# A channel gate that is guessed early: flag and branch ahead of ScalarE's last waits, an early gate from 44 rows, four slots of 68 rows, 512-wide sums

## The chip, the cores and the metric

The kernel runs on one core of one Trainium2 chip. The metric is the device time of one execution in microseconds, as the median of ten runs; beside them stands one profiled execution, whose trace is read here.

## The reference

`x` has the shape 1 x 384 x 384 x 384 (height, width, channels) in bf16, `w1d` has one element. Cut to what matters, for a one-element filter:

```python
g = jnp.einsum("bhwc->bc", x) / (H * W)     # mean of each channel
s = sigmoid(g * w1d[0])                     # one gate per channel
return x * s[:, None, None, :]              # every pixel times its channel's gate
```

The mean needs all of `x`, and the product needs all of `x` again: 113.25 MB are read and 113.25 MB written if `x` is read once.

## The kernel before, in words

**Guess, then check.** A core's on-chip memory does not hold `x`. The kernel therefore computes a gate `s_early` from the first rows alone, multiplies every row with it as the rows pass through, and goes on summing. At the end it computes the true gate `s_true` from the sum of everything and compares both as bf16 bit patterns (`not_equal`, a maximum over the channels, a cast to the integer `redo`). If they differ anywhere, a second pass reads `x` again and multiplies with `s_true`. With these inputs they are the same, and the second pass is branched over.

**Rows and tiles.** A "row" is 128 pixels, one to a partition, with 384 channels in each: 768 bytes per partition. There are 1,152 rows. They are cut into 26 tiles, eight of 45 rows and eighteen of 44 (`split(n_rows, TILE)`). A tile's transfer has one contiguous piece per partition (34,560 or 33,792 bytes), so 128 pieces, which are shared by the core's 16 DMA engines. Partition p holds pixels that follow each other in memory.

**The arena.** What is left of the on-chip memory, 209,344 bytes per partition or 272 rows, is the arena. The class `Ring` hands out places in it one after the other; six tiles fit. A tile that needs a place in use first has the oldest tile gated and stored (`put`).

**What each engine does for a tile.**
- SyncE issues the load (`load`, through `plan.dma`, line 91).
- TensorE adds the rows up over the partitions: one matmul per row with a matrix of ones, 384 columns wide, accumulated in one PSUM bank (`add_rows`, line 206): bank `acc0` for the first three tiles, `acc1` for the others.
- VectorE multiplies the tile in place with the gate (`gate`, line 165).
- ScalarE issues the store (`put`, through `plan.dma`).

After the third tile VectorE copies the sum to `total` (line 249) and ScalarE computes `s_early` (line 255). After the last tile's gate VectorE adds the second bank (line 267), ScalarE computes `s_true` (line 273), and VectorE makes the flag (lines 281, 289, 295).

**Order and waits.** The class `Planner` writes one stream of instructions for each engine, in the order in which `plan.op` and `plan.dma` are called, and puts in the waits: before an operation the engine waits for the writer of what it reads, and for the writer and readers of what it overwrites (line 99). Each DMA has a semaphore of a pool of 50. An engine works through its stream in that order. So where a step stands in the code decides what stands ahead of it in its engine's stream.

**The end.** SyncE, VectorE and ScalarE each call `second_pass`: wait for the flag, load it into a register (line 326), branch (line 327). ScalarE first waits for all stores (lines 345 and 346) and raises `stored`, for which the other engines would wait inside the branch. Line 322 stands for the block's end, where all engines meet.

Of the kernel before, what the change touches and what calls it, by code (L numbers as in the profile page):

```python
# [3 lines left out]
P = 128  # L4
ROW = 384
BF16 = mybir.dt.bfloat16
F32 = mybir.dt.float32
U16 = mybir.dt.uint16
I32 = mybir.dt.int32
ACT_F = mybir.ActivationFunctionType  # L10
ALU = mybir.AluOpType


class Planner:
# [9 lines left out]
    def __init__(self, nc, name, n_dma_sems):  # L24
        self.nc = nc
        self.streams = {e: [] for e in ("sync", "scalar", "vector", "tensor", "gpsimd")}
        self.sems = {e: nc.alloc_semaphore(f"{name}_{e}") for e in self.COMPUTE}
        self.count = {e: 0 for e in self.COMPUTE}
        self.pool = [nc.alloc_semaphore(f"{name}_dma_{i}") for i in range(n_dma_sems)]
        self.pool_uses = [0] * n_dma_sems  # L30
        self.n_dma = 0
        self.writer = {}
        self.readers = {}
        self.seen = {e: {} for e in self.streams}
        self.final = []
# [70 lines left out]
def split(n, most):  # L106
    k = -(-n // most)
    return [n // k + (i < n % k) for i in range(k)]


class Ring:


    def __init__(self, size):
        self.size, self.at = size, 0

    def take(self, n):
        if self.at + n > self.size:
            self.at = 0
        self.at += n  # L120
        return self.at - n


TILE = 45
AHEAD_TILES = 3


def bass_standalone__channel_attn_eca__vision_kernel(
# [3 lines left out]
    out: bass.AP,  # L132
):
    B, H, W, C = x.shape
    assert B == 1 and C == ROW and (B * H * W) % P == 0
    n_rows = B * H * W // P
    x_rows, o_rows = x.flatten_outer_dims(), out.flatten_outer_dims()

    def dram(view, r0, n):
        return view[r0 * P : (r0 + n) * P, :].rearrange("(p t) c -> p (t c)", p=P)  # L140

    ones = nc.alloc_sbuf_tensor("ones", [P, P], BF16)
    s_early = nc.alloc_sbuf_tensor("s_early", [P, C], BF16)
    s_true = nc.alloc_sbuf_tensor("s_true", [P, C], BF16)
    w_one = nc.alloc_sbuf_tensor("w_one", [1, 16], BF16)
    w_scaled = nc.alloc_sbuf_tensor("w_scaled", [P, 2], F32)
    warm = nc.alloc_sbuf_tensor("warm", [P, 2], F32)
    wrong = nc.alloc_sbuf_tensor("wrong", [P, 1], F32)
    redo = nc.alloc_sbuf_tensor("redo", [P, 1], I32)
    total = nc.alloc_sbuf_tensor("total", [P, C], F32)  # L150
    n_arena = nc.sbuf_bytes_remaining // (2 * C)
    arena = nc.alloc_sbuf_tensor("arena", [P, n_arena * C], BF16)
    acc = [nc.alloc_psum_tensor(f"acc{i}", [P, 512], F32) for i in range(3)]

    def at(r0, n):
        assert r0 + n <= n_arena
        return arena[:, r0 * C : (r0 + n) * C]

    def rows(r0, n):
        return [("sb", r) for r in range(r0, r0 + n)]  # L160

    def gate(place, n, s):
        s_b = s[:].unsqueeze(1).broadcast_to([P, n, C])
        v = at(place, n).rearrange("p (t c) -> p t c", t=n)
        return lambda e: e.tensor_tensor(v, v, s_b, ALU.mult)  # L165

    sizes = split(n_rows, TILE)
    early_rows = sum(sizes[:AHEAD_TILES])
    plan = Planner(nc, "a", 50)


    plan.op("gpsimd", lambda e: e.memset(warm[:, 0:1], 0.0), writes=["warm"])  # L172
    plan.op("vector", lambda e: e.memset(ones[:], 1.0), writes=["ones"])  # L173
    plan.dma("scalar", w_one[0:1, 0:1], w1d.unsqueeze(0), writes=["w_one"])
    plan.op(
        "scalar",
        lambda e: e.activation(warm[:, 1:2], warm[:, 0:1], ACT_F.Sigmoid),  # L177
        reads=["warm"],
        writes=["warm1"],
    )  # L180
    plan.op(
        "tensor",
        lambda e: e.matmul(  # L183
            acc[2][:, 0:1], ones[0:1, :], w_one[0:1, 0:1], start=True, stop=True
        ),
        reads=["ones", "w_one"],
        writes=["acc2"],
    )
    for i, n in enumerate((early_rows, n_rows)):
        plan.op(  # L190
            "vector",
            lambda e, i=i, n=n: e.tensor_scalar_mul(  # L192
                w_scaled[:, i : i + 1], acc[2][:, 0:1], 1.0 / float(P * n)
            ),
            reads=["acc2"],
            writes=[f"w_scaled{i}"],
        )

    def load(place, n, r0):
        plan.dma("sync", at(place, n), dram(x_rows, r0, n), writes=rows(place, n))  # L200

    def add_rows(place, n, bank, first, last):
        for i in range(n):
            plan.op(
                "tensor",
                lambda e, i=i: e.matmul(  # L206
                    acc[bank][:, :C],
                    ones[:],
                    at(place + i, 1),
                    start=first and i == 0,  # L210
                    stop=last and i == n - 1,
                ),
                reads=["ones"] + (rows(place, n) if i in (0, n - 1) else []),
                writes=[f"acc{bank}"],
                signal=i == n - 1,
            )

    def put(place, n, r0):
        plan.op(
            "vector",  # L220
            gate(place, n, s_early),
            reads=["s_early"] + rows(place, n),
            writes=rows(place, n),
        )
        plan.final.append(
            plan.dma("scalar", dram(o_rows, r0, n), at(place, n), reads=rows(place, n))
        )


    ring = Ring(n_arena)  # L230
    inside = []
    r0 = 0
    for k, n in enumerate(sizes):
        place = ring.take(n)
        while inside and any(
            p < place + n and place < p + m for p, m, _ in inside
        ):
            put(*inside.pop(0))
        load(place, n, r0)
        inside.append((place, n, r0))  # L240
        if k < AHEAD_TILES:
            add_rows(place, n, 0, k == 0, k == AHEAD_TILES - 1)
        else:
            add_rows(place, n, 1, k == AHEAD_TILES, k == len(sizes) - 1)
        r0 += n
        if k == AHEAD_TILES - 1:
            plan.op(
                "vector",
                lambda e: e.tensor_copy(total[:], acc[0][:, :C]),  # L249
                reads=["acc0"],  # L250
                writes=["total"],
            )
            plan.op(
                "scalar",
                lambda e: e.activation(  # L255
                    s_early[:], total[:], ACT_F.Sigmoid, scale=w_scaled[:, 0:1]
                ),
                reads=["total", "w_scaled0", "warm1"],
                writes=["s_early"],
            )  # L260
    for tile in inside:
        put(*tile)


    plan.op(
        "vector",
        lambda e: e.tensor_tensor(total[:], total[:], acc[1][:, :C], ALU.add),  # L267
        reads=["total", "acc1"],
        writes=["total"],
    )  # L270
    plan.op(
        "scalar",
        lambda e: e.activation(  # L273
# [2 lines left out]
        reads=["total", "w_scaled1"],  # L276
        writes=["s_true"],
# [6 lines left out]
        reads=["s_true", "s_early"],  # L284
        writes=["total"],
# [4 lines left out]
        reads=["total"],  # L290
        writes=["wrong"],
# [4 lines left out]
        reads=["wrong"],  # L296
        writes=["redo"],
# [2 lines left out]


    again = Planner(nc, "b", 50)
    ring = Ring(n_arena)
    r0 = 0
    for n in sizes:
        place = ring.take(n)
        again.dma("sync", at(place, n), dram(x_rows, r0, n), writes=rows(place, n))
        again.op(
            "vector",
            gate(place, n, s_true),  # L310
            reads=rows(place, n),
            writes=rows(place, n),
        )
        again.final.append(
            again.dma("scalar", dram(o_rows, r0, n), at(place, n), reads=rows(place, n))
        )
        r0 += n
    for token in again.final:
        again._wait("scalar", token)
    stored = nc.alloc_semaphore("stored")  # L320

    with nc.Block() as block:

        def second_pass(name, e):
            e.wait_ge(*checked)
            flag = e.value_load(redo[0:1, 0:1], min_val=0, max_val=1)
            with e.If(flag > 0):
                if name != "scalar":
                    e.wait_ge(stored, 1)
                again.emit(name, e)  # L330

        @block.sync
        def _(e):
            plan.emit("sync", e)
            second_pass("sync", e)

        @block.vector
        def _(e):
            plan.emit("vector", e)
            second_pass("vector", e)  # L340

        @block.scalar
        def _(e):
            plan.emit("scalar", e)
            for token in plan.final:
                e.wait_ge(*token)
            e.sem_inc(stored, 1)
            second_pass("scalar", e)

        @block.tensor  # L350
        def _(e):
            plan.emit("tensor", e)

        @block.gpsimd
        def _(e):
            plan.emit("gpsimd", e)
# [28 lines left out]
```

## Time and profile before

| | us |
|---|---|
| median of 10 runs | 533.87 (533.58 to 535.16) |
| the profiled execution's own time | 533.52 |
| its span, first to last instruction | 531.6 |
| TensorE matmuls busy | 245.5 |
| VectorE busy | 236.7 |
| first gate computed (`s_early` starts) | 45.1 |
| first store issued | 54.9 |
| last load issued | 455.1 |
| last store issued | 503.0 |
| flag made (cast starts) | 505.3 |

The profiled execution is one run; its span is the time between its first and last instruction on the core. Busy times are sums over the span. "Q" after an engine's name (SPq, ACTq) means its sequencer, which issues transfers, waits and branches. q1 is the queue of the transfers that SyncE issues, q10 that of ScalarE, q8 the one through which TensorE's instructions arrive. A transfer "lands" when its last semaphore update is seen. A packet in the trace's records is one contiguous piece of a transfer on one DMA engine.

### The profile page before, as it was taken

How to read it: one execution, taken by the hardware profiler on the slowest of the kernel's cores; microseconds unless marked ns; L12 is line 12 of the kernel's file. 1: busy time of each engine (PE TensorE's matmuls, PEld its weight loads, DVE VectorE, ACT ScalarE, POOL GpSimd, SP SyncE). 2: the span in 40 equal slices, each digit the busy share in tenths (PEclk: the TensorE clock that was granted, in tenths of full speed). 3: DMA queues.
4: the chain of work that ended last, by engine and by line, in shares of the span. 5: the costliest groups of instructions: out<-in, count | busy, mean ns of one | idle time of the engine just before them, and what ended most of it. 6: DMA issues, size and time to landing. Idle time of an engine off the chain costs nothing.

```text
span 531.6 us, 2500 instructions
## 1 busy us (share of the span) xinstructions
PE 245.5 (46%) x1153; PEld 128.5 (24%) x1153; DVE 236.7 (45%) x34; ACT 2.7 (1%) x4; POOL 0.3 (0%) x5
## 2 busy tenths in 40 slices
PE   0879643337247256246156256266156156265100
PEld 0435311123123123123023023133023033033000
DVE  0005999561651642651642642632642642633700
ACT  1000000000000000000000000000000000000000
POOL 0000000000000000000000000000000000000000
PEclk9989867577576576687686776677686786775655
DMA  9999999999999999999999999999999999999996
GB/s 372 419 451 421 412 419 452 419 439 428 440 423 445 422 443 419 442 432 426 442 432 422 447 428 425 445 422 433 442 422 437 440 418 440 440 420 441 435 423 272
DMA packets 7501, 226.66 MB, mean 426 GB/s; under 512 B 834, under 2 KB 834, under 8 KB 834
## 3 DMA queue, kind: packets, MB, share of 16 engines
q1 hardware_dynamic: 3744, 113.25, 49.6%
q10 hardware_dynamic: 3746, 113.25, 49.4%
q8 instruction: 9, 0.15, 0.1%
q14 instruction: 2, 0.02, 0.0%
HBM read 113.25 MB, written 113.25 MB: 426 GB/s over the span
## 4 chain that ended last, share of the span: by engine, by line
another core or an unknown queue 63%; DMA 19%; DVE 7%; PE 4%; SPq 1%; issue 1%; ACT 0%; DVEq 0%
DMA arena<-in_x_dram 12%; DMA out_dram<-arena 8%; DVE arena L165 7%; PE acc L206 4%; SPq L91 1%; ACT s_true L273 0%; ACT s_early L255 0%; DVE total L281 0%; DVE total L249 0%; DVE wrong L289 0%; DVE total L267 0%; SPq L99 0%; DVE redo L295 0%; DVEq L99 0%
## 5 line engine op out<-in xcount | busy, mean ns | idle before, releaser
L206 PE MATMUL acc<-arena,ones 128*128 128x384 bf16 x1152 | 245.4, 385 | 246.3 <-DMA arena<-in_x_dram 246.3
L165 DVE TENSOR_TENSOR arena<-arena,s_early 128x16896 bf16<-128x16896 bf16 (+1 forms) x26 | 234.1, 9018 | 223.8 <-PE acc L206 223.1
L206 PEld LDWEIGHTS acc<-arena,ones 128*128 128x128 bf16 x1152 | 128.4, 113 | 362.9 <-DMA arena<-in_x_dram 256.0
L249 DVE COPY total<-acc 128x384 f32<-128x384 f32 x1 | 0.6, 556 | 42.0 <-PE acc L206 42.0
L273 ACT ACTIVATE s_true<-total,w_scaled 128x384 bf16<-128x384 f32 x1 | 0.6, 614 | 457.7 <-DVE total L267 457.7
L177 ACT ACT_TABLE_LOAD x1 | 1.3, 1283 | 1.3 <-PEq L370 1.3
L183 PE MATMUL acc<-w_one,ones 1*128 1x1 bf16 x1 | 0.2, 158 | 2.0 <-DMA w_one<-in_w1d_dram 2.0
L281 DVE TENSOR_TENSOR total<-s_true,s_early 128x384 f32<-128x384 uint16 x1 | 0.6, 557 | 0.7 <-ACT s_true L273 0.7
L255 ACT ACTIVATE s_early<-total,w_scaled 128x384 bf16<-128x384 f32 x1 | 0.6, 614 | 42.3 <-DVE total L249 42.3
L192 DVE TENSOR_SCALAR w_scaled<-acc 128x1 f32<-128x1 f32 x2 | 0.2, 152 | 1.3 <-PE acc L183 1.3
L183 PEld LDWEIGHTS acc<-w_one,ones 1*128 1x128 bf16 x1 | 0.1, 98 | 2.0 <-issue 2.0
L289 DVE TENSOR_REDUCE wrong<-total 128x1 f32<-128x384 f32 x1 | 0.6, 552 | 0.0
L267 DVE TENSOR_TENSOR total<-total,acc 128x384 f32<-128x384 f32 x1 | 0.5, 547 | 0.0
L173 DVE MEMSET ones<- 128x128 bf16 x1 | 0.2, 165 | 0.8 <-PEq L370 0.8
L177 ACT ACTIVATE warm<-warm 128x1 f32<-128x1 f32 x1 | 0.2, 203 | 0.0
L295 DVE CAST redo<-wrong 128x1 int32<-128x1 f32 x1 | 0.2, 153 | 0.0
L370 POOL MEMSET const-bfloat16-1.0<- 128x1 bf16 x1 | 0.1, 102 | 0.0
L370 POOL MEMSET const-uint8-127<- 128x1 uint8 x1 | 0.1, 102 | 0.0
L172 POOL MEMSET warm<- 128x1 f32 x1 | 0.1, 99 | 0.3 <-POOLq L370 0.3
L370 POOL MEMSET const-float32-0.0<- 128x1 f32 x1 | 0.1, 99 | 0.2 <-issue 0.2
L370 POOL MEMSET const-float32-1.0<- 128x1 f32 x1 | 0.1, 99 | 0.0
## 6 DMA issues: line engine op xcount, KB each, us to landing
arena<-in_x_dram SPq DMA_DIRECT2D x18, 4224.0 KB, 28.3
out_dram<-arena ACTq DMA_DIRECT2D x18, 4224.0 KB, 72.9
arena<-in_x_dram SPq DMA_DIRECT2D x8, 4320.0 KB, 30.9
out_dram<-arena ACTq DMA_DIRECT2D x8, 4320.0 KB, 57.6
w_one<-in_w1d_dram ACTq DMA_DIRECT2D x1, 0.0 KB
```

Source lines behind the costliest of these rows:

```text
L91: ("op", lambda e: e.dma_start(out, in_), self.pool[i], 16)
L165: return lambda e: e.tensor_tensor(v, v, s_b, ALU.mult)
L177: lambda e: e.activation(warm[:, 1:2], warm[:, 0:1], ACT_F.Sigmoid),
L183: lambda e: e.matmul(acc[2][:, 0:1], ones[0:1, :], w_one[0:1, 0:1], start=True, stop=True),
L206: lambda e, i=i: e.matmul(acc[bank][:, :C], ones[:], at(place + i, 1), start=first and i == 0, stop=last and i == n - 1,),
L249: lambda e: e.tensor_copy(total[:], acc[0][:, :C]),
L255: lambda e: e.activation(s_early[:], total[:], ACT_F.Sigmoid, scale=w_scaled[:, 0:1]),
L267: lambda e: e.tensor_tensor(total[:], total[:], acc[1][:, :C], ALU.add),
L273: lambda e: e.activation(s_true[:], total[:], ACT_F.Sigmoid, scale=w_scaled[:, 1:2]),
L281: lambda e: e.tensor_tensor(total[:], s_true[:].bitcast(U16), s_early[:].bitcast(U16), ALU.not_equal),
L289: lambda e: e.reduce_max(wrong[:], total[:], axis=mybir.AxisListType.X),
L370: nc = _bacc.Bacc("TRN2", target_bir_lowering=False, num_devices=1)
```

## The change

1. **ScalarE's end.** `second_pass` comes directly after ScalarE's planned stream: it waits for the flag, loads it and branches. The waits for the last stores follow the branch, and stand also inside its body, ahead of raising `stored`.
2. **The early gate** is computed from the first tile alone, which has 44 rows, and not from three tiles of 45.
3. **Tiles and places.** `Ring` is gone. The arena has slots of 68 rows (`SLOT`), tile k goes to slot k modulo the number of slots. The tiles are 44 rows, then fifteen of 68, then two of 44: 18 tiles. A tile is put when all slots are taken.
4. **Wide sums.** A matmul takes 512 columns (`WIDE`) across the borders of rows: 33 matmuls for 44 rows, 51 for 68. They go in turn to three banks, so a bank's columns are channels in one of three shifted orders. `add_banks` brings them together in six VectorE operations for a group (128 to 384 columns each); there are two groups, the first tile and all others.
5. **The first two loads** are issued in halves, one by SyncE and one by ScalarE. In ScalarE's stream the half of the first tile comes first, then the small load of the weight, then the activation that warms the table up, then `s_early`, then the half of the second tile.
6. **The weight's product** with ones goes to a PSUM bank of its own, and its steps (`weight`) stand behind the first loads.

```diff
-TILE = 45
-AHEAD_TILES = 3
+WIDE = 512
+EDGE, SLOT = 44, 68
...
-    sizes = split(n_rows, TILE)
-    early_rows = sum(sizes[:AHEAD_TILES])
+    n_slots = n_arena // SLOT
+    full, rest = divmod(n_rows - EDGE, SLOT)
+    if rest < EDGE:
+        full, rest = full - 1, rest + SLOT
+    sizes = [EDGE] + [SLOT] * full + [4 * q for q in split(rest // 4, EDGE // 4)]
...
-    def load(place, n, r0):
-        plan.dma("sync", at(place, n), dram(x_rows, r0, n), writes=rows(place, n))
+    def load(place, n, r0, queues=("sync",)):
+        of = dram(x_rows, r0, n)
+        i = 0
+        for queue, m in zip(queues, split(n, -(-n // len(queues)))):
+            plan.dma(
+                queue,
+                at(place + i, m),
+                of[:, i * C : (i + m) * C],
+                writes=rows(place + i, m),
+            )
+            i += m
+
+    def add_rows(place, n, group, first, last):
+
+        n_wide = n * C // WIDE
+        start = place * C
+        for i in range(n_wide):
+            bank = acc[group][i % 3]
             plan.op(
                 "tensor",
-                lambda e, i=i: e.matmul(
-                    acc[bank][:, :C],
+                lambda e, i=i, bank=bank: e.matmul(
+                    bank[:, :],
                     ones[:],
-                    at(place + i, 1),
-                    start=first and i == 0,
-                    stop=last and i == n - 1,
+                    arena[:, start + i * WIDE : start + (i + 1) * WIDE],
+                    start=first and i < 3,
+                    stop=last and i >= n_wide - 3,
                 ),
...
+    def add_banks(group, copy):
+
+        for m, lo, hi in ((0, 0, C), (0, C, WIDE), (1, 0, 256), (1, 256, WIDE),
+                          (2, 0, P), (2, P, WIDE)):
+            c = (128 * m + lo) % C
+            part = total[:, c : c + hi - lo]
+            of = acc[group][m][:, lo:hi]
+            if copy and (m, lo) == (0, 0):
+                emit = lambda e, part=part, of=of: e.tensor_copy(part, of)
+            else:
+                emit = lambda e, part=part, of=of: e.tensor_tensor(
+                    part, part, of, ALU.add
+                )
+            plan.op("vector", emit, reads=[f"acc{group}", "total"], writes=["total"])
...
+    def weight():
+
+        plan.dma("scalar", w_one[0:1, 0:1], w1d.unsqueeze(0), writes=["w_one"])
+        plan.op(
+            "scalar",
+            lambda e: e.activation(warm[:, 1:2], warm[:, 0:1], ACT_F.Sigmoid),
...
     for k, n in enumerate(sizes):
-        place = ring.take(n)
-        while inside and any(
-            p < place + n and place < p + m for p, m, _ in inside
-        ):
+        place = k % n_slots * SLOT
+        if len(inside) == n_slots:
             put(*inside.pop(0))
-        load(place, n, r0)
+        load(place, n, r0, ("sync", "scalar") if k < 2 else ("sync",))
         inside.append((place, n, r0))
-        if k < AHEAD_TILES:
-            add_rows(place, n, 0, k == 0, k == AHEAD_TILES - 1)
+        if k == 0:
+            weight()
+            add_rows(place, n, 0, True, True)
         else:
-            add_rows(place, n, 1, k == AHEAD_TILES, k == len(sizes) - 1)
+            add_rows(place, n, 1, k == 1, k == len(sizes) - 1)
         r0 += n
-        if k == AHEAD_TILES - 1:
...
+        if k == 0:
+            add_banks(0, copy=True)
             plan.op(
                 "scalar",
                 lambda e: e.activation(
...
             with e.If(flag > 0):
-                if name != "scalar":
+                if name == "scalar":
+                    for token in plan.final:
+                        e.wait_ge(*token)
+                    e.sem_inc(stored, 1)
+                else:
                     e.wait_ge(stored, 1)
                 again.emit(name, e)
...
         def _(e):
             plan.emit("scalar", e)
+            second_pass("scalar", e)
             for token in plan.final:
                 e.wait_ge(*token)
-            e.sem_inc(stored, 1)
-            second_pass("scalar", e)
```

## The prediction

> **What bounds the kernel now.** I read the page's busy shares first, then its slices, then a table of windows, then the chain and the queue waits, and last the source view of the flag's lines.
>
> The page's engine line, its two DMA rows and its queue part:
>
> ```profile
> PE 245.5 (46%) x1153; PEld 128.5 (24%) x1153; DVE 236.7 (45%) x34; ACT 2.7 (1%) x4; POOL 0.3 (0%) x5
> DMA  9999999999999999999999999999999999999996
> GB/s 372 419 451 421 412 419 452 419 439 428 440 423 445 422 443 419 442 432 426 442 432 422 447 428 425 445 422 433 442 422 437 440 418 440 440 420 441 435 423 272
> q8 instruction: 9, 0.15, 0.1%
> HBM read 113.25 MB, written 113.25 MB: 426 GB/s over the span
> ```
>
> No engine is busy half the time; the transfers are busy in all slices but the last. The windows (length, engines, clock, DMA share, GB/s):
>
> ```profile
> 13.90:54.90 41.00, 33.69 (x180) 18.56 (x180) 9.71 (x3) 0.61 (x1) 0.00 (x0) 0.96 1.00 431
> 77.00:455.00 378.00, 180.27 (x832) 93.61 (x830) 177.53 (x21) 0.00 (x0) 0.00 (x0) 0.71 1.00 433
> 503.00:524.00 21.00, 0.00 (x0) 0.00 (x0) 1.66 (x4) 0.61 (x1) 0.00 (x0) 0.50 1.01 434
> 524.00:529.50 5.50, 0.00 (x0) 0.00 (x0) 0.00 (x0) 0.00 (x0) 0.00 (x0) 0.50 0.44 190
> 529.50:531.60 2.10, 0.00 (x0) 0.00 (x0) 0.00 (x0) 0.00 (x0) 0.00 (x0) 0.50 0.00 0
> ```
>
> Loads alone (to 54.9), loads with stores, and stores alone all run at 431 to 434 GB/s. So an earlier first store is worth nothing in itself. Time is lost only where the 16 DMA engines stand still: before the first packet at 1.75 us, in the ragged end after 524, and in the last 2.1 us.
>
> The chain (start, length) and SyncE's queue wait show what starts a load in the steady part:
>
> ```profile
> 73.08 40.83 DMA out_dram<-arena
> 113.92 0.02 SPq L99
> 113.96 0.33 SPq L91
> SPq L99 <- DMA out_dram<-arena: 443.8, 20, 73.2
> ```
>
> Every later load waits for the store that frees its place; that is free as long as another transfer is queued meanwhile. The tail, by the source views of the flag, the branch and the block's end:
>
> ```profile
> L326 ACTq TENSOR_LOAD <-redo x1: 472/472/472, 530.1 to 530.1; - x1
> L326 ACTq FUSED_REGOPS  x1: 169/169/169, 530.6 to 530.6; - x1
> L327 ACTq COMPARE_BRANCH  x1: 54/54/54, 530.9 to 530.9; - x1
> L322 ACTq DRAIN  x1: 78/78/78, 531.4 to 531.4; - x1
> ```
>
> The last store lands at 529.93 (landing records). ScalarE then loads the flag, branches and reaches the block's end only at 531.36.
>
> **A ledger of one DMA engine**, from the packet records. A 33,792 B packet starts 1.247 us after the one before, a 34,560 B packet 1.2755 us: the same rate per byte, nothing per packet. Eight partitions of a row thus cost an engine 0.2267 us. First packet 1.75, + 0.76 because first loads take 1.7 to 2.3 us for 1.28, + 2,304 rows x 0.2267 = 522.3, + 0.76 at the first store (22 loads stretched at 56 to 58 us), + 0.3 for 52 semaphore packets, + 0.35 scattered = 526.2. Seven engines do end near 526.1. The last packet ends at 529.47: each fetch of instructions (q8, nine of them) holds one engine 0.95 us and the next packet 0.4 us, and the late engine has about two of them and a late start.
>
> **What the Trainium skill says.** "DMA: Bandwidth & Descriptors", "Issuing engines are not separate DMA queues": a second issuing engine saves sequencer time alone. The trace agrees: one queue gives 431, two give 433 GB/s; the split loads get nothing for it. The same page, "Queues, rings and completion order": an engine takes its queues in turn, packet by packet. Agrees: load and store packets alternate one by one on each engine. "Runtime: NRT & Kernel Launch", "Instruction fetch mechanics": instructions come in 16 KiB blocks of 256. Agrees: nine fetches for 2,306 TensorE instructions. "Advanced Engine Details and Errata", "Control Flow Timing": about 108 ns for a compare-and-branch. The trace has 54 ns, but 0.42 us more to the next instruction; I use the trace.
>
> **The change, part by part.** Tiles are now 44, fifteen of 68, 44, 44 rows. 209,344 B remain for the arena, or 272 rows: exactly four slots. I call loads L0 to L17 and stores S0 to S17.
>
> *The tail.* Flag load, register steps and branch move from behind the last landing to behind the check. From 530.07 (the waits' end) to 531.36 is **-1.3 us**. Their new cover: the flag comes about 5 us after S17's issue (six adds from PSUM, about 2.5 us from 0.55 us for 384 columns and 0.15 for one; then 0.6 + 0.6 + 0.55 + 0.15), the load and branch 1.5 us later; S17 needs at least 1.1 + 10 + 0.4 us. Nothing but the final waits is queued behind the new wait on ScalarE. Without the cover it would cost the same 1.3.
>
> *Operations.* TensorE streams the same columns, 864 x 512 for 1,152 x 384; VectorE the same elements at 0.53 ns. Neither binds: nothing. A longer packet gives nothing (ledger); 14 fewer pairs of semaphores give 0.1. TensorE's instructions fall from 2,306 to about 1,730: **six fetches** for nine, so no engine should get two. The weight's small load stands behind half of L0 on ScalarE's queue and lands with it: nothing.
>
> *The second half of L1.* In ScalarE's order it stands behind the s_early activation, which waits for L0, its sums and six VectorE adds. ScalarE is in order: a wait for old stores that stands behind the s_true activation ran only when that had started, at 503.44. So: L0 lands at 13, TensorE to 22 (9.57 us for 45 rows), adds 2.7: the half of L1 is issued at about 25 and not at 3. There its 26,112 B packets alternate with L2's of 52,224 and get a third of the rate: 8 x (1.93 + 0.96) = 23 us and the packets already taken, landing at about 52. TensorE takes L1 to 64, VectorE (26,112 x 0.53 ns = 13.8 us) to 78: **S1 comes at 78**. Before, its like came at 64.0.
>
> *S0 and the gap.* The gate of 44 rows issues S0 at 34 and not 54.9, but S0 queues behind that half of L1, and L4 needs S0's slot. With L0 to L3 and S0, 44 + 204 + 44 = 292 rows, all that is queued has been moved: 1.75 + 0.76 + 0.76 + 292 x 0.2267 = 69.5. S1 is eight us away, L4 may start only when S0 has landed on the slowest engine. In the kernel before, a sixth place and a store every 9 us closed this. **The DMA engines run dry.** Slowest engine: 0.85 later (first loads landed 13.07 to 13.93) to 1.7 (33.56 to 35.29 with a fetch on one); I take 1.3. Landing 0.4, SyncE's wait and issue to first packet 1.1 (0.74 to 1.75 at the start): L4 starts at 72.3, with 0.76 of first-packet delay again. Gap: 72.3 + 0.76 - 69.5 = 3.5 us, bounds 2.8 and 4.3. After it the backlog holds: L4 is there until S1 comes, S2 at 92 before S1 is through.
>
> *The end of transfers.* 73.0 + 2,012 rows x 0.2267 (456.1) + 0.5 = 529.6; the slowest engine adds one fetch, 1.3, and 0.4 of spread: 531.3 against 529.47: **+1.8**.
>
> *Two unknowns.* A first packet on an idle ScalarE queue stretched the loads by 0.76 at 56 us; a queue that rejoined at 77 us cost nothing. For L1's half: 0 to 0.76, I take 0.3. Last tile: after S13 has landed about 54 us of transfers remain ahead of S17, while L17's landing (28 by the page's median, 33 with the longer packets), TensorE 10, VectorE 9 and issue 1.1 take 48 to 53: S17 is just in time. I take 0.3, bounds 0 and 4.
>
> **Sum**: -1.3 + 1.8 + 0.3 + 0.3 = +1.1. On the profiled execution: 533.52 us, span 531.6, so 1.9 lie around it; after, span 532.7, time 534.6. The median of the runs shown is 0.35 above that execution: 533.87 + 1.1 = **535.0**. About 0.2%, 1.07 us, is what a measurement of this kernel can tell from no change.
>
> **Rivals.** *No gap, faster* (0.20): if turns are shared by bytes and not by packets, L1's half ends near 45, S0 lands before L3 and L4 joins in time. Then one fetch for two on the slowest engine gives -1.3, the tail -1.3: 531.3. The point: S0 landed before L3. Against it stand the alternating packets; but those had equal sizes. *A cheap gap, same* (0.28): 2.8 us, neither unknown: -1.3 + 1.1 = -0.2, 533.7. *Last tile late, slower* (0.08): TensorE at half clock (0.74 now) takes 14.7 us for 44 rows, S17 is some 3 late: 537.5. *The tail stays* (0.05): if the branch moved but ScalarE's end is no shorter, 1.3 is missing: 536.3. A second pass is no rival: both gates round to the same number (the largest arguments are 3e-6 and 1e-6).
>
> **How the numbers follow.** The likeliest is the full gap (0.39), 534.9 to 536.3 by itself; it is a narrow call beside the cheap gap. Faster 0.20, same 0.28, slower 0.39 + 0.08 + 0.05 = 0.52. The range, 531.0 to 537.0, takes in all but the late tile's far end and the best of the gapless case.
>
> **What would show it.** Right: no DMA packet for 2 to 3 us near 70 us; L1's half issued at about 25, S1 at about 78; six q8 packets; ScalarE's flag load near S17's issue, and under 1 us from the last landing to its DRAIN. Wrong: no hole at 70 (the no-gap rival), a hole near 517 (the late tile), or a last packet under 529.5.

## The result, and the profile after

The changed kernel takes **537.63 us** (median of 9 runs, 535.36 to 538.89) against 533.85 (30 runs, 533.32 to 535.16): 1.0066 of the time before, 95% interval 1.0056 to 1.0076. It is slower, by 3.5 us by the ratio and 3.8 us by the medians, where 1.1 was forecast, and above the range. Its profiled execution took 536.88 us, with a span of 534.9. In the ratios here and below, runs more than 1.5% above the fastest of their kernel are left out; the medians hold every run.

The page of the changed kernel, the rows that answer to those shown of before:

```profile
PE 221.0 (41%) x848; PEld 91.7 (17%) x865; DVE 239.7 (45%) x36; ACT 2.7 (1%) x4; POOL 0.3 (0%) x5
DMA  8999889999999999999999999999999999999997
GB/s 357 467 437 437 368 332 379 435 437 437 433 437 437 437 433 435 437 433 430 430 439 430 437 430 422 430 437 435 433 437 433 437 435 438 413 437 442 424 400 327
q8 instruction: 7, 0.11, 0.1%
HBM read 113.25 MB, written 113.25 MB: 423 GB/s over the span
```

The transfers still run at 430 to 440 GB/s nearly everywhere, but slices 5 to 7 (53 to 94 us) have 368, 332 and 379, and the last two are thin. The windows of the changed kernel cut those places out (length, engines, clock, DMA share, GB/s):

```profile
53.00:69.50 16.50, 15.56 (x64) 6.79 (x66) 2.67 (x1) 0.00 (x0) 0.00 (x0) 0.87 0.99 407
69.50:72.40 2.90, 2.85 (x14) 1.31 (x14) 2.90 (x1) 0.00 (x0) 0.00 (x0) 1.00 0.03 12
80.00:85.00 5.00, 4.95 (x24) 2.27 (x24) 5.00 (x2) 0.00 (x0) 0.00 (x0) 1.00 1.04 334
100.00:455.00 355.00, 145.48 (x551) 60.07 (x562) 159.26 (x12) 0.00 (x0) 0.00 (x0) 0.71 1.00 433
520.20:522.70 2.50, 0.00 (x0) 0.00 (x0) 2.43 (x4) 0.00 (x0) 0.00 (x0) 0.50 0.38 162
533.50:534.90 1.40, 0.00 (x0) 0.00 (x0) 0.00 (x0) 0.00 (x0) 0.00 (x0) 0.50 0.00 0
```

Three different losses are seen here. From 69.5 to 72.4 the DMA engines do nothing (share 0.03). From 80 to 85 they are busy all the time (1.04) and yet move only 334 GB/s: by the packet records, each engine has one load packet there that takes 3.0 to 3.6 us, where 1.93 is usual. From 520.2 to 522.7 most engines have run dry again (0.38). In between, over 355 us, 433 GB/s flow as before: the steady part lost nothing.

The timeline of the changed kernel shows how the first hole comes about (start, length):

```profile
27.47 0.61 ACT L272 ACTIVATE s_early<-total,w_scaled 128x384 bf16<-128x384 f32 x1 [24.23 <-DVE total L210]
27.48 0.35 ACTq L91 DMA_DIRECT2D arena<-in_x_dram  x1
53.88 34.83 PE L188 MATMUL acc<-arena,ones 128*128 128x512 bf16 x150 [29.18 <-DMA arena<-in_x_dram]
66.83 41.10 DVE L156 TENSOR_TENSOR arena<-arena,s_early 128x26112 bf16<-128x26112 bf16 x3 [29.75 <-PE acc L188]
```

ScalarE issues its half of L1 10 ns after the early gate's activation has started, at 27.48 us. The half lands at 53.75 and TensorE, idle for 29 us, begins to sum L1; VectorE gates L1 from 66.83, and S1 is issued at 80.62. S0 had landed at 71.41 and L4 was issued at 71.49; its first packet came at 72.45.

The tail, by the source views of the flag and of the block's end in the changed kernel:

```profile
L337 ACTq TENSOR_LOAD <-redo x1: 1093/1093/1093, 526.5 to 526.5; - x1
L333 ACTq DRAIN  x1: 8/8/8, 534.7 to 534.7; - x1
```

The flag is loaded at 526.5, eight us ahead of the last landing (534.46); from that landing to the end of the span are 0.49 us, where there were 1.72.

### The profile page after: what moved, and what is told of

It reads as the page before. It is cut to its first block, busy times and chain, and to the rows that moved or that the text cites. A ratio compares the mean times of both kernels' runs of the same rounds, so it can differ in the third digit from the quotient of the medians.

```text
span 534.9 us, 1879 instructions
## 1 busy us (share of the span) xinstructions
PE 221.0 (41%) x848; PEld 91.7 (17%) x865; DVE 239.7 (45%) x36; ACT 2.7 (1%) x4; POOL 0.3 (0%) x5
## 4 chain that ended last, share of the span: by engine, by line
another core or an unknown queue 62%; DMA 21%; DVE 7%; PE 6%; issue 1%; SPq 1%; ACT 0%; ACTq 0%; DVEq 0%
DMA arena<-in_x_dram 11%; DMA out_dram<-arena 7%; DVE arena L156 6%; PE acc L188 6%; DMA w_one<-in_w1d_dram 3%; DVE total L210 1%; SPq L91 1%; ACT s_true L285 0%; DVE total L293 0%; DVE total L208 0%; DVE wrong L301 0%; ACTq L91 0%; SPq L99 0%; PE w_all L237 0%
## 5 line engine op out<-in xcount | busy, mean ns | idle before, releaser
L156 DVE TENSOR_TENSOR arena<-arena,s_early 128x26112 bf16<-128x26112 bf16 (+1 forms) x18 | 233.1, 12957 | 261.3 <-PE acc L188 260.6
L188 PE MATMUL acc<-arena,ones 128*128 128x512 bf16 x847 | 220.9, 425 | 276.6 <-DMA arena<-in_x_dram 274.6
L188 PEld LDWEIGHTS acc<-arena,ones 128*128 128x128 bf16 x864 | 91.6, 108 | 405.4 <-DMA arena<-in_x_dram 251.9
L210 DVE TENSOR_TENSOR total<-total,acc 128x128 f32<-128x128 f32 (+2 forms) x11 | 4.5, 407 | 0.3
## 6 DMA issues: line engine op xcount, KB each, us to landing
arena<-in_x_dram ACTq DMA_DIRECT2D x1, 3264.0 KB, 26.3
```

What stands on the lines that cost most here:

```text
L188: lambda e, i=i, bank=bank: e.matmul(bank[:, :], ones[:], arena[:, start + i * WIDE : start + (i + 1) * WIDE], start=first and i < 3, stop ...
L210: emit = lambda e, part=part, of=of: e.tensor_tensor(part, part, of, ALU.add)
```

## The experiments

Each table row is one kernel; the kernel before ran beside it on the same chip, at medians of 533.83 to 534.0. The last column counts the runs over 535 us; of the 132 runs of the kernel before that ran beside these kernels, 4 are over 535, the highest at 539.66. Where the runs of a kernel scatter, its ratio and its median need not agree closely. The letters that stand for theories are explained in the expectations: G is the gap at 70 us, E the end, S the four large slots, H the start, F the early first store.

| kernel | median us | lowest to highest | ratio to before, 95% interval | over 535 |
|---|---|---|---|---|
| l1_half_first | 533.77 | 530.40 to 538.27 | 0.9998, 0.9975 to 1.0021 | 9 of 22 |
| last_24 | 536.52 | 535.14 to 540.55 | 1.0050, 1.0028 to 1.0073 | 15 of 15 |
| half_first_last_24 | 534.48 | 530.49 to 539.80 | 0.9999, 0.9978 to 1.0021 | 11 of 22 |
| flag_first | 532.67 | 532.32 to 533.51 | 0.9974, 0.9963 to 0.9985 | 0 of 22 |
| places_68 | 537.84 | 536.41 to 541.35 | 1.0089, 1.0064 to 1.0114 | 6 of 6 |
| six_places | 532.05 | 531.57 to 540.25 | 0.9986, 0.9966 to 1.0005 | 2 of 14 |
| six_places_narrow | 532.34 | 531.90 to 539.58 | 0.9970, 0.9959 to 0.9981 | 1 of 8 |
| early_45 | 534.96 | 533.30 to 546.13 | 1.0040, 1.0018 to 1.0062 | 11 of 22 |
| six_places_gate3 | 531.53 | 531.29 to 532.27 | 0.9959, 0.9946 to 0.9972 | 0 of 5 |
| taper | 534.29 | 531.81 to 539.56 | 1.0027, 1.0003 to 1.0051 | 6 of 14 |
| l1_on_sync | 532.67 | 530.67 to 539.59 | 0.9983, 0.9968 to 0.9998 | 2 of 14 |
| changed_again | 537.25 | 535.90 to 540.07 | 1.0077, 1.0056 to 1.0098 | 6 of 6 |

### The half of L1: l1_half_first and l1_on_sync

```diff
-        load(place, n, r0, ("sync", "scalar") if k < 2 else ("sync",))
+        if k != 1:
+            load(place, n, r0, ("sync", "scalar") if k < 2 else ("sync",))
...
             weight()
+            load(SLOT, sizes[1], n, ("sync", "scalar"))
```

> The changed kernel with one step moved: ScalarE issues its half of the second load ahead of the early gate's activation instead of behind it. Theory G (the loss is the hole at 70 us: S1 comes late because that half-load is late, and L4 has to wait for S0 with nothing else queued): the hole of 3.0 us with its 0.75 us of first-packet delay and the 1.3 us by which loads are stretched when S1 starts on an idle queue all go; about 5 us faster than the changed kernel, 532.5 us, and no hole near 70 us. Theory E (the loss is made at the end: the last store is issued at 522 us, after the store ahead of it has run out on most engines): no change, 537.5 us, or the freed time shows as a longer hole near 517 us. Theory S (four large slots are worse in the steady part): no change.

The windows of l1_half_first at the same places:

```profile
69.50:72.40 2.90, 0.00 (x0) 0.00 (x0) 2.90 (x1) 0.00 (x0) 0.00 (x0) 0.50 1.12 486
80.00:85.00 5.00, 4.95 (x23) 2.26 (x23) 0.00 (x0) 0.00 (x0) 0.00 (x0) 0.99 0.99 428
```

Both losses at the start are gone: the share is full at 70 us, and 428 GB/s flow at 80 us. The half is issued at 1.80 us, S1 at 59.3. The engines that are not late have finished the store ahead of the last at 515.4 us, against 520.3: 4.9 us. The hole (2.95), the first packets after it (0.75) and the stretch at 82 us (1.3) make 5.0. The median falls by 3.9 us, though the runs are far apart.

```diff
-        load(place, n, r0, ("sync", "scalar") if k < 2 else ("sync",))
+        load(place, n, r0, ("sync", "scalar") if k < 1 else ("sync",))
```

> The changed kernel with the second load whole on SyncE's queue; only the first is split. If a second issuing engine is worth nothing and the hole came from where the half stood in ScalarE's order: the hole at 70 us goes and the time is that of the kernel with the half issued early, some 4 us under the changed kernel. If the split was worth something for itself: slower than that.

> The changed kernel as it is, on the same chip as the three others, for the comparison: a median of 537 to 538 us, the runs spread over 3 us or more.

On one chip the changed kernel took 537.25 us and l1_on_sync 532.67: **4.6 us from one digit**. Its window from 69.5 to 72.4 us is full (first line). It has no hole at the end either (second line), where l1_half_first still has one (third line), so a part of the 4.6 may be that hole's:

```profile
69.50:72.40 2.90, 0.00 (x0) 0.00 (x0) 2.90 (x1) 0.00 (x0) 0.00 (x0) 0.50 1.17 504
515.50:518.00 2.50, 0.00 (x0) 0.00 (x0) 2.23 (x6) 0.06 (x1) 0.00 (x0) 0.50 1.01 433
515.50:518.00 2.50, 0.00 (x0) 0.00 (x0) 2.43 (x4) 0.00 (x0) 0.00 (x0) 0.50 0.53 230
```

So theory G holds, and the cause is shown twice: l1_half_first keeps the half on ScalarE's queue and moves only its place, l1_on_sync takes it off that queue, and both lose the hole and about 4 us. A second engine that issues a part of L1 brought nothing that could be measured (532.67 without it, 533.77 with it); the split of L0 stayed in both and was not tested.

### The branch alone: flag_first

```diff
             plan.emit("scalar", e)
+            second_pass("scalar", e)
             for token in plan.final:
                 e.wait_ge(*token)
-            e.sem_inc(stored, 1)
-            second_pass("scalar", e)
```

(The waits and `stored` also stand inside the branch's body, as in the change.)

> The kernel before with the first part of the change alone: ScalarE loads the flag and branches ahead of its waits for the last stores. From the profiles, 1.72 us from the last landing to the end of the span before and 0.49 us in the changed kernel: 1.2 us faster than before, 532.6 us. If the branch's end is not what sets the time (the engines' meeting or something outside the span does), no change, 533.85 us.

Measured 532.67 against 533.93: 1.26 us faster by the medians, within 0.1 of what the profiles gave; the ratio's interval allows 0.8 to 2.0. The source views of flag_first:

```profile
L326 ACTq TENSOR_LOAD <-redo x1: 822/822/822, 506.0 to 506.0; - x1
L322 ACTq DRAIN  x1: 8/8/8, 530.6 to 530.6; - x1
```

The flag's load took 0.82 us here and 0.47 at the end of the kernel before; it is hidden by 24 us of stores.

### The end: last_24, half_first_last_24 and taper

```diff
-    sizes = [EDGE] + [SLOT] * full + [4 * q for q in split(rest // 4, EDGE // 4)]
+    sizes = [EDGE] + [SLOT] * full + [rest - 24, 24]
```

> The changed kernel with other sizes of the last two tiles: 64 and 24 rows instead of 44 and 44. TensorE and VectorE then need some 10 us instead of 19 from the last landing to the last store's issue. Theory E: the hole of up to 2.5 us near 522 us goes; the slowest engine had none of it in the profiled execution, so 0 to 1.5 us faster in the median (536 to 537.6 us), and the runs, which spread over 3.5 us, come closer together. Theory G: the hole at 70 us stays, so not under 535.5 us. Theory S: no change.

> Both edits of the two kernels before together. Theory G with E: no hole at 70 us and none near the end, 531.5 to 532.5 us, faster than the kernel before by about 1.5 us, of which 1.25 is the branch moved. Theory S: still over 535 us with neither hole, the loss being spread over the steady part.

The taper has, with the half early:

```diff
+    sizes = [EDGE] + [SLOT] * 13 + [64, 56, 44, 36, 24]
```

> The changed kernel with ScalarE's half of the second load early and with last tiles that grow smaller step by step (64, 56, 44, 36, 24 rows in place of two of 68 and two of 44), so that each of the last stores is ready before the one ahead of it has run out. Theory G with E: neither the hole at 70 us nor one near the end; the fastest runs at 529 to 530.5 us, the median 1 us or more under that of the kernel with the early half alone, if the hole at the end cost anything there; the scatter stays. If the hole at the end lies only on engines that are ahead: the median as with the early half alone.

The windows of last_24:

```profile
69.50:72.40 2.90, 2.85 (x14) 1.27 (x13) 2.90 (x1) 0.00 (x0) 0.00 (x0) 1.00 0.03 12
512.40:516.20 3.80, 0.00 (x0) 0.00 (x0) 2.95 (x8) 0.61 (x1) 0.00 (x0) 0.50 1.05 453
```

last_24 has no hole at the end and keeps the one at 70 us. Its median, 536.52, lies 0.7 to 1.1 us under the changed kernel's 537.25 and 537.63, and its runs lie no closer together: theory E's narrower scatter failed. half_first_last_24 has another hole instead, of up to 2.5 us at 505 to 507.8, because its tile of 64 rows is now the late one. taper was to have no hole, but by the packet records most engines stand still from 520.0 to 522.2 us, 1.3 us in the mean, because the last store is issued at 521.3; with 534.29 it is no faster than l1_half_first with 533.77. So taper does not show what a kernel with neither hole takes. In the changed kernel's profile the hole lay on engines that were ahead; the engine that ended last began S17 without a wait. By the pairs with and without it (the changed kernel and last_24, l1_half_first and l1_on_sync), the hole is worth about 1 us at most, less than the runs scatter.

### The other parts: places_68, six_places, six_places_narrow, early_45

```diff
-TILE = 45
-AHEAD_TILES = 3
+TILE = 68
+AHEAD_TILES = 2
```

> The kernel before with its tile size alone changed: 68 and 67 rows instead of 45 and 44, so four places in the arena instead of six, and the early gate from two tiles (136 rows instead of 134). Open is why the runs of the four-slot kernels lie up to 8 us apart, with and without the hole at 70 us, where those of the kernel before lie within 1.5 us. Theory S (four large places let the DMA engines drift apart: a load starts when the slowest engine has finished a store, and the others have fewer transfers to fall back on): slower than 534.5 us and scattered over 3 us or more. Theory H (the scatter comes from the start of the changed kernel, the split loads and the early gate): 533.9 us, scattered no more than before; the 5 or 9 fewer transfers are worth nothing.

Slower by 4.0 us and scattered: what theory S said, but its profile names a plainer cause for a part of the loss. A timeline line and a window of places_68:

```profile
501.73 13.56 DVE L165 TENSOR_TENSOR arena<-arena,s_early 128x25728 bf16<-128x25728 bf16 x1 [16.97 <-PE acc L206]
511.50:516.20 4.70, 0.00 (x0) 0.00 (x0) 4.25 (x2) 0.42 (x1) 0.00 (x0) 0.50 0.21 88
```

The last tile of 67 rows needs 27 us of TensorE and VectorE, so its store comes at 515.3, when most engines have had nothing to do for 3 to 4.7 us (share 0.21). Here even the last engine waited, 1.3 us from its last packet to the next. The changed kernel's last tiles of 44 rows make that wait shorter: on its last engine there was none. What the rest of the 4.0 us is was not found.

```diff
-EDGE, SLOT = 44, 68
+EDGE, SLOT = 44, 44
...
+    full, rest = divmod(n_rows, SLOT)
+    sizes = [SLOT] * full + [rest]
...
```

(The half of L1 is issued early here too, by the edit of l1_half_first.)

> The changed kernel with ScalarE's half of the second load issued early, and with six places of 44 rows instead of four of 68: 26 tiles of 44 rows and a last one of 8. Theory S: the scatter goes (within 1.5 us), no hole anywhere, and the time is that of the kernel before less the 1.25 us of the branch and up to 1.3 us of instruction fetches: 531.3 to 532.7 us. Theory H: still scattered over 3 us or more.

> The kernel of the run before with sums of 384 columns in one bank per group, as in the kernel before, and one VectorE operation in place of six. If the wide sums matter only through TensorE's instructions (nine fetches instead of seven, each holding one DMA engine 1.3 us): 0 to 1.3 us slower than with wide sums. If TensorE's speed mattered: more. If neither: the same within 0.3 us.

With six places 9 of 14 runs lie at 531.6 to 532.3 us, but the other five at 534.0 to 540.3: theory S explains a part of the scatter at best. Sums of 384 columns in place of 512 give 532.34 for 532.05: 0.3 us, the small end of what was expected and not clear of the scatter. Of the wide sums nothing more can be told.

```diff
-AHEAD_TILES = 3
+AHEAD_TILES = 1
```

> The kernel before with the early gate from its first tile alone (45 rows) instead of three. The first store is issued at about 34 us instead of 55. Since the transfers are busy from the first packet either way: the same, 533.9 us within 0.5. If an earlier first store were worth what it moves forward: up to 20 us faster. If the first tiles' gates come so early that stores and loads share the start and a load then waits: slower, with a hole near 70 us.

The fastest runs, 533.3 us, are those of the kernel before: a first store 20 us earlier (34.3 for 54.9) is worth nothing. There is no hole. But the runs reach to 546 us, 11 of 22 are over 535 where none of the 37 runs of the kernel before beside them is, and the median is 1.1 us worse: this edit alone brings the scatter.

### Late first store, six places: six_places_gate3

```diff
-            add_rows(place, n, 0, True, True)
...
+        if k < 3:
+            add_rows(place, n, 0, k == 0, k == 2)
...
-        if k == 0:
+        if k == 2:
             add_banks(0, copy=True)
...
```

(This is cut to what differs from six_places; the early gate's divisor counts three tiles, too.)

> Six places of 44 rows, ScalarE's half of the second load early, wide sums and the branch first, as in the earlier run of six places, but with the early gate from three tiles again (132 rows), so that the first store comes at about 54 us instead of 36. Theory F (an early first store leaves the store queue short and the load queue long, and lets one DMA engine drift away from the others in some runs): the scatter of the earlier run (531.6 to 540.3 us) goes; all runs within 1.5 us around 531.5 to 532.0 us, the best version. If the scatter has another cause (the split loads, the wide sums): several of the runs still over 534 us.

531.53 us with all five runs within 1 us: the fastest kernel measured here, 2.5 us under the 534.0 of the kernel before beside it (0.9959, 0.9946 to 0.9972). Its first store comes at 53.2 us. That fits theory F, but does not show it: the same kernel with the gate from one tile had 9 undisturbed runs of 14, and at that rate five in a row come about one time in nine.

**What stays open** is what starts the scatter. Two scattered executions were caught in profiles. In that of six_places_narrow (539.58 us) no DMA engine idles before 515 us, yet a store's landings on the first and the last engine grow from 1.7 us apart to 10.6, and between 100 and 490 us 107 load packets are over 60 ns longer than usual (none in the kernel before, 1 in six_places at 532.0). In that of half_first_last_24 (537.01 us) the landings grow from 1.6 us apart to 11.1, with 25 such packets, and at the end one engine alone is 5 us behind all others. In the kernel before they stay at 3.1 to 3.7 us from 90 us on. So one or a few engines fall behind while they load, with four places and with six. It came in kernels whose first store is early and in places_68, whose first store is not (53 such packets, but landings only 4.0 us apart), and the kernel before has a few runs of the kind (4 of 132 over 535); why the order of stores and loads should bring it was not found.

## Why the prediction was wrong, point by point

The hole at 70 us was foreseen, with its cause. What failed is two terms of the sum: the stretch of the packets, which was priced at 0.3 us and laid on L1's half, and came as 1.3 us at the start of S1; and the lateness of the slowest engine, priced at 1.7 us, measured 3.1.

**Right.** *The tail*: -1.3 forecast, -1.23 by the profiles and -1.26 by flag_first. *The mechanism of the loss*: the half of L1 behind the activation, forecast at 25 us and found at 27.48 (the weight's load landed at 14.98 and held TensorE up for 1.7 us, which had been priced at nothing); landing 52, found 53.75; S1 78, found 80.6. *The hole*: dry from 69.5 (69.5), first packet of L4 72.3 (72.45), first-packet delay 0.76 (0.75). *No worth in* the early gate, the second issuing engine for L1 and the wide sums: early_45, l1_on_sync and six_places_narrow bear it out; for the larger packets the rate per byte does (33,792 B after 1.247 us, 52,224 B after 1.924). *The steady part* untouched: 433 GB/s in both.

**Wrong, and by which terms.** The forecast of the profiled execution was 534.6, it took 536.88: 2.3 us are missing.

- *The stretch, +1.3 for 0.3.* The prediction saw the loads of the kernel before stretched at 56 us, took it for the cost of a first packet on an idle queue, and feared it for L1's half. That half caused none. S1 did: 16 load packets of 3.0 to 3.6 us for 1.93. The table below shows that the idle queue was the wrong reading.
- *Packets, -0.6.* 52,224 B packets follow each other after 1.924 us, not 1.927. With the 1.3 the engines that are on time would come to 530.35 (S16 at 520.3 and 10.05 for S17), had they not waited for S17; forecast 529.6: +0.75.
- *The slowest engine, +1.4.* "One fetch, 1.3, and 0.4 of spread": 1.7 forecast, **3.1 measured** (533.46 against 530.35). TensorE's instructions came in seven fetches, not six, and the saving on the last engine did not come; before, it was 3.4. Which engine took which fetch, the packet records do not say.
- *The last tile, 0 for 0.3.* S17 was issued at 521.84, just too late for most engines, but the last engine had no wait.
- *The last landing, +0.55, in no term.* It came 1.0 us after the end of the last packet (534.46 and 533.45), where before it came after 0.46 and in l1_half_first after 0.45. Why was not found.

Together, 0.75 (the engines on time), 1.4 (the slowest), 0.55 (the landing) and 0.07 (the tail) make 2.8; less the two times 0.3 that the sum had added, 2.2 of the 2.3 us are found. The rest of the error is the scatter, which no term had: this profiled execution lies 0.75 us under the median of its runs, where 0.35 was added.

What starts, while the engines carry loads alone, and what it does to the load packets in flight, from the packet records:

| kernel | what starts | ScalarE's queue until then | packets, us, for usual | extra us per engine |
|---|---|---|---|---|
| before | S0 | idle | 1.7 to 2.1 for 1.28 | 0.7 |
| changed | L1's half, a load | idle since 15 us | 1.93 for 1.93 | 0.0 |
| changed | S0 | L1's half, just ended | 2.6 to 2.8 for 1.93 | 0.8 |
| changed | S1 | idle since 71 us | 3.0 to 3.6 for 1.93 | 1.3 |
| l1_half_first | S0 | idle | 2.5 to 2.8 for 1.93 | 0.7 |
| l1_on_sync | S0 | idle | 2.1 to 3.5 for 1.93 | 1.5 |

An idle queue was neither enough (L1's half) nor needed (S0 of the changed kernel). In all five cases with a stretch a store starts where only loads are in flight. The kernels without the misplaced half pay that once, with S0; those with it (the changed kernel and last_24) pay it twice, because S0 has gone when S1 comes. In l1_half_first S1 starts at 59.3 us while S0 is still under way, and nothing is stretched. That is a reading of the traces; no experiment moved a store's start alone, and why its size differs was not found.

**On medians.** flag_first takes 1.26 us off, and the misplaced half adds 3.9 (l1_half_first) to 4.6 (l1_on_sync): from 533.85 that gives 536.5 to 537.2, against 537.63 and 537.25 measured. l1_on_sync and flag_first have the same median, 532.67: without the misplaced half, all of the rest of the change together brought nothing in the median.

The rival with a cheap gap was right in the gap and its place, but its price was too low; the rival without a gap fell: unequal packets do take turns one by one, so L1's half with its smaller packets needed 26.3 us.

## What to carry to other kernels

When transfers set the time, ask of every DMA that is moved or split what stands ahead of it in its issuing engine's order: a load behind an activation that waits cost 3.9 to 4.6 us, and the split of L1 itself saved nothing that could be measured. Count at each moment what is still queued until the next wait is released; a kernel runs dry where the answer is nothing, and here the first packets after the hole cost 0.75 us again, and the next store, which found loads alone, 1.3 us. A wait that is only bookkeeping, as the flag and branch here, can go behind the last transfers' cover: that part alone made the kernel 1.26 us faster.

## What the runs showed of the hardware that had not been expected

A store that started while the engines carried loads alone stretched the loads in flight: by 0.7 us per engine in the kernel before, by 0.8 at 53 us and 1.3 at 83 us in the changed one; a load that was issued to an idle queue at 27.5 us stretched none. An instruction fetch of 16 KiB held one DMA engine about 0.93 us, and the packet behind it took 0.4 us more. And an earlier first store, with nothing else changed, spread the runs from 1.6 us to 13 us.
